# Lightning attention into a switch-routed MoE: order of the q, k and v loads, the first step in head halves, and the lists emptied in two parts

## The chip, the cores and the metric

The kernel runs on one core of one Trainium2 chip. The metric is the time of one execution on the device in microseconds, the median of several runs. The engines are TensorE (PE; its weight loads are PEld), VectorE (DVE), ScalarE (ACT), GpSimd (POOL) and SyncE (SP), and each takes its instructions in order. Transfers are issued from the queues of SyncE, ScalarE and GpSimd.

## The reference, cut to what matters

```python
# lightning attention: batch 4, heads 8, sequence 768, head size 64, blocks of 64, all f32
for b in range(nb):
    intra = (qb @ kb.T * Dmask) @ vb            # Dmask = lam ** (i - j) for i >= j
    inter = (qb * lam_pow) @ kv_state
    out[:, :, block b] = intra + inter
    kv_state = lam_block * kv_state + (kb * rev_pow).T @ vb
x = out as (4 * 768, 8 * 64)                    # 3072 tokens of 512
# switch routing, top 1 of 8 experts, hidden size 1024
expert = argmax(x @ w_gate); gate_w = softmax(x @ w_gate)[expert]
y[tokens of e] = gate_w * (relu(x[tokens of e] @ w1[e]) @ w2[e])
```

## The kernel before, in words

**Attention.** The kernel works with blocks of 128 positions, so there are `NSTEP` = 6 of them, and with two batches at a time: twelve steps (n, b) with b = 0 or 2. For a step it loads q, k and v as tiles of 128 positions by 2 batches by 8 heads by 64, 0.524 MB each (`q_in`, `k_in`, `v_in`, three buffers each). `turn_q` and `turn_k` transpose one half of the heads at a time on TensorE into `tq` and `tk`; ScalarE copies them out as `qT` and `kT`; from n = 1 on VectorE also makes `qsT` (q with its decay), and GpSimd makes `kd` (k with its decay). `score` multiplies kT and qT into `sp`, and VectorE multiplies by the decay mask into `mt`. `attend_states` adds the part of the state (`op<-qsT,st`), `grow` makes the state's growth (`cp<-v_in,kd`), `attend` multiplies v and mt (`op<-mt,v_in`), `to_sbuf` copies out to `xT`, `update` adds `cp` to the state with the faded state `sd` that `fade` makes on GpSimd.

**Order.** `enter` takes a step in (loads for a later step, then its transposes), `leave` makes the logits and the rows of a finished step. An iteration of the main loop with step i as `cur` does: `leave` of step i-1, `enter` of step i+1, then states, `grow` and `attend` of step i, `score` of step i+1, the routing of a finished group of four batches, `fade`, and `store_places`. The first step is entered and scored ahead of the loop, and the second is entered inside the first iteration after its attention.

**Loads.** `load` issues q, k, v of one step on SyncE's queue; the first two steps are loaded at the start, and `enter(n, b)` loads step (n+1, b), which is two steps on. The very first q and k go as one transfer per batch.

**Routing lists.** `slots` in DRAM holds for each of 8 experts R = 3456 entries of 16 bytes. `empty_lists` fills it once, in iteration 1, with one transfer of 432 KB from GpSimd's queue. When a group of 512 tokens is ranked, `put` makes each token's place and `store_places` writes entries with indirect transfers from GpSimd, two in an iteration (`slots<-entry,slot_i`). Later SyncE reads lists back, GpSimd gathers the rows of x and TensorE runs the experts; that is two thirds of the time.

**What fixes the order.** The instruction planner (Tile) puts the instructions of each engine in an order by its own estimate of when they are ready. `pin` keeps an instruction behind the one traced before it on its engine: transposes and products on TensorE, `kd`, `sd`, the puts and the emptying on GpSimd are pinned; the loads of q, k and v, the copies qT and kT, and the mt products are not.

Of the kernel before, what the change touches and what calls it, by code (L numbers as in the profile page):

```python
# [10 lines left out]
F32 = mybir.dt.float32  # L11
BF16 = mybir.dt.bfloat16
I32 = mybir.dt.int32
# [9 lines left out]
def kernel(  # L23
# [29 lines left out]
    nc = tc.nc  # L53
    B, H, S, D = q.shape
    N, MD = out.shape
    E = moe_w_gate.shape[1]
    F = moe_w1.shape[2]
    P = 128
    C = P
    NSTEP = S // C  # L60
# [26 lines left out]

    def load(n, b0, first=False):

        got = [qkv.tile([P, 2, H, D], F32, tag=name, name=f"{name}_in") for name in "qkv"]  # L90
        for t, src in zip(got, (q, k, v)):
            per = 1 if first and src is not v else 2
            for b in range(0, 2, per):
                nc.sync.dma_start(  # L94
                    out=t[:, b:b + per].rearrange("p b h d -> p (b h) d"),
                    in_=src[b0 + b:b0 + b + per, :, n * C:(n + 1) * C, :].rearrange(
                        "b h s d -> s (b h) d"))
        return got

# [3 lines left out]
    nc.scalar.dma_start(out=lam_bc, in_=lam.partition_broadcast(P))  # L103
    loaded = {(0, 0): load(0, 0, True), (0, 2): load(0, 2)}
    ident = const.tile([P, P], F32, name="ident")
# [94 lines left out]
    def pin(inst):  # L200
        tc.keep_in_program_order(inst)
# [10 lines left out]
    def turn_q(m, s):  # L212
        shp = turned_shape
        tq = turned(m.q, s, bank(2 * s, shp, "tq"))
        qT = work.tile(shp, F32, tag="qT", name="qT")
        nc.scalar.copy(qT, tq)
        m.qT.append(qT)
# [219 lines left out]

    empty = ffn.tile([P, E * R // P, ENTRY], I32, tag="xg", name="empty", bufs=4)
    nc.gpsimd.memset(empty, 0)
# [423 lines left out]

    def empty_lists():

        pin(nc.gpsimd.dma_start(out=slots.rearrange("(p r) c -> p (r c)", p=P),
                                in_=empty.rearrange("p r c -> p (r c)").bitcast(F32)))
        pin(nc.gpsimd.dma_start(out=xs[0, :].rearrange("(c p) -> c p", c=DC), in_=zeros[:DC, :]))

# [7 lines left out]

    def enter(n, b, between=nothing):
        if n + 1 < NSTEP:
            loaded[n + 1, b] = load(n + 1, b)  # L880
        m = SimpleNamespace(n=n, b=b, qT=[], qsT=[], kT=[], kd=[], mt=[])
        m.q, m.k, m.v = loaded[n, b]

        for s, turn_one in (((0, turn_q), (1, turn_q), (0, turn_k), (1, turn_k)) if not (n or b)
                            else ((0, turn_q), (0, turn_k), (1, turn_q), (1, turn_k))):
            turn_one(m, s)
            between()
            between = nothing
        return m

# [21 lines left out]
    def give_places(group):  # L912

        waiting.append((group, put(*group), 0))
# [68 lines left out]

    order = [(n, b) for n in range(NSTEP) for b in range(0, B, 2)]
    cur, last = enter(*order[0]), None
    for s in range(2):
        score(cur, s)

    pin(nc.scalar.dma_start(out=gates[0][:, :, :E],
                            in_=moe_w_gate.rearrange("(c p) e -> p c e", p=P)))  # L990
    for u in range(2):
        nc.gpsimd.tensor_copy(gates[1][halves[u]], gates[0][halves[1 - u]])
    for i in range(len(order)):
        rest = leave(last, (4, 6, 7) if i < len(order) - 1 else (4, 2, 3)) if last else nothing

        ahead = enter(*order[i + 1], rest) if 0 < i < len(order) - 1 else None
        if ahead:
# [21 lines left out]
        if i == 0:  # L1019
            ahead = enter(*order[1])  # L1020
        update(cur)
# [9 lines left out]
        for group in ranked:  # L1031
            give_places(group)
        if ahead:
            fade(ahead)
            store_places()
        if i == 1:
            empty_lists()
        last, cur = cur, ahead
# [139 lines left out]
```

## Time and profile before

| | us |
|---|---|
| median of 3 runs | 458.72 |
| the runs | 458.73, 458.72, 456.27 |
| the profiled execution's own time | 458.06 |
| its span | 455.6 |
| TensorE busy | 432.8 (95%) |
| VectorE, ScalarE, GpSimd busy | 265.8, 180.7, 251.4 |
| mean granted clock of TensorE | 0.991 of full speed |

The span is the stretch from the first to the last instruction that the profile has; the execution's own time is 2.5 us longer. Busy time of TensorE is modelled at the ends of its products. A wait is put down to what came last by the profile, as in `[1.49 <-DMA k_in<-in_k_dram]`: idle for 1.49 us until a transfer into k_in had landed. On the timeline an SPq line is the issue of a transfer on SyncE's queue, not its landing.

### The profile page before, as it was taken

The numbers are of one execution on the slowest core, as the hardware profiler recorded it, in microseconds if no ns is written. First come the engines' busy times: TensorE is split into PE (matmuls) and PEld (weight loads), VectorE is DVE, ScalarE is ACT, GpSimd is POOL, SyncE is SP. The second block draws the span as 40 slices with busy tenths as digits, with TensorE's granted clock in tenths as the row PEclk, the third lists the DMA queues.
The fourth block names the chain that finished last, engine by engine and source line by source line (L and its number), as shares of the span: only waits on it lengthen the run. The fifth ranks groups of instructions, "written<-read, shape, count | busy, mean of one in ns | idle before, by whom it ended". The sixth has DMA issues, their size and how long they took to land.

```text
span 455.6 us, 9420 instructions
## 1 busy us (share of the span) xinstructions
PE 432.8 (95%) x3713; PEld 370.5 (81%) x3713; DVE 265.8 (58%) x590; ACT 180.7 (40%) x327; POOL 251.4 (55%) x203
## 2 busy tenths in 40 slices
PE   4989999998979999999999999999999999999993
PEld 3778888887857885996898799689879979979973
DVE  2756566582737543557546944864773784485453
ACT  3455445553522033634255252524515525423301
POOL 4234455533143558756766484586659569548203
PEclk9999999998989999999999999999999999999999
DMA  9999999999561995956294277729529739201001
GB/s 171 206 266 237 212 253 214 233 207 228 189 232 48 305 287 104 372 92 251 67 260 161 101 236 90 255 67 254 202 72 270 166 115 267 51 1 66 2 12 60
DMA packets 123207, 78.39 MB, mean 172 GB/s; under 512 B 104556, under 2 KB 104560, under 8 KB 123153
## 3 DMA queue, kind: packets, MB, share of 16 engines
q1 hardware_dynamic: 114176, 58.13, 53.0%
q0 software_dynamic: 5040, 13.25, 9.3%
q10 hardware_dynamic: 3936, 6.31, 4.1%
q8 instruction: 31, 0.51, 0.5%
q14 instruction: 24, 0.19, 0.2%
HBM read 58.96 MB, written 13.16 MB: 158 GB/s over the span
## 4 chain that ended last, share of the span: by engine, by line
PE 89%; DMA 4%; SPq 3%; DVE 1%; issue 1%; another core or an unknown queue 1%; ACT 0%; POOL 0%; POOLq 0%; DVEq 0%
PE p L678 28%; PE p L722 22%; PE p L730 10%; PE ph L560 5%; PE sp L244 4%; PE op L278 4%; PE po L836 4%; SPq L94 3%; PE tx L339 2%; PE op L269 2%; PE cp L303 2%; DMA k_in<-in_k_dram 2%; DMA q_in<-in_q_dram 2%; PE tk L209 2%; PE tq L209 1%; PE lgT L329 1%
## 5 line engine op out<-in xcount | busy, mean ns | idle before, releaser
L690 ACT ACTIVATE hT<-hT 128x408 f32<-128x408 f32 (+4 forms) x56 | 29.5, 527 | 68.5 <-DVE hT L687 68.4
L250 DVE TENSOR_TENSOR mt<-sp,decay 128x512 f32<-128x512 f32 x48 | 30.4, 685 | 22.0 <-PE sp L244 21.9
L428 POOL DMA_INDIRECT slots<-entry,slot_i x24 | 23.5, 981 | 33.7 <-DVE slot_i L426 15.1
L678 PE MATMUL p<-xgT,w1t 128*128 128x204 f32 (+4 forms) x224 | 41.5, 328 | 0.0
L234 POOL TENSOR_TENSOR kd<-k_in,kdec 128x512 f32<-128x512 f32 x20 | 20.4, 1038 | 35.0 <-PE cp L303 18.3
L678 PEld LDWEIGHTS p<-xgT,w1t 128*128 128x128 f32 x224 | 37.6, 190 | 1.2 <-issue 0.9
L489 POOL DMA_INDIRECT out_dram<-o,list x22 | 22.5, 1021 | 25.4 <-ACT o L810 20.4
L608 POOL TENSOR_TENSOR s_k<-w1t 128x1024 f32<-128x1024 f32 x7 | 16.6, 2367 | 28.1 <-DMA across<-planes_k 11.8
L608 POOL TENSOR_TENSOR s_q<-w1t 128x1024 f32<-128x1024 f32 x7 | 16.5, 2360 | 28.0 <-PE p L730 16.9
L722 PE MATMUL p<-w2t,hT 128*128 128x256 f32 x128 | 29.7, 381 | 0.0
L483 POOL DMA_INDIRECT xg<-xs,list x24 | 24.7, 1029 | 6.4 <-issue 5.8
L722 PEld LDWEIGHTS p<-w2t,hT 128*128 128x128 f32 x128 | 23.9, 190 | 5.3 <-issue 2.5
L687 DVE TENSOR_TENSOR hT<-p,u_qsT 128x408 f32<-128x408 f32 (+4 forms) x28 | 15.8, 563 | 21.1 <-PE p L678 21.1
L244 PE MATMUL sp<-qT,kT 64*128 64x128 f32 x384 | 25.8, 281 | 0.2 <-ACT kT L228 0.2
L730 PE MATMUL p<-w2t,hT 128*64 128x256 f32 x112 | 25.7, 382 | 0.0
L278 PE MATMUL op<-mt,v_in 128*64 128x128 f32 x384 | 24.9, 284 | 0.0
L244 PEld LDWEIGHTS sp<-qT,kT 64*128 64x128 f32 x384 | 22.8, 187 | 2.6 <-issue 1.7
L574 DVE TENSOR_TENSOR u_kT<-p,u_qT 128x408 f32<-128x408 f32 (+4 forms) x14 | 7.9, 563 | 27.2 <-PE p L678 27.1
L560 PE MATMUL ph<-xgT,w1t 128*128 128x256 f32 (+1 forms) x128 | 23.5, 341 | 0.0
L278 PEld LDWEIGHTS op<-mt,v_in 128*64 128x64 f32 x384 | 22.6, 144 | 0.3 <-ACT kT L228 0.2
L730 PEld LDWEIGHTS p<-w2t,hT 128*64 128x64 f32 x112 | 14.8, 137 | 9.4 <-issue 2.3
L810 ACT ACTIVATE o<-o,list 128x512 f32<-128x512 f32 (+2 forms) x7 | 5.1, 722 | 43.7 <-DVE o L807 43.7
(214 smaller groups left out, 1129.1 us busy)
## 6 DMA issues: line engine op xcount, KB each, us to landing
w2t<-in_moe_w_dram SPq DMA_DIRECT2D x8, 2048.0 KB
w1t<-in_moe_w_dram SPq DMA_DIRECT2D x7, 2048.0 KB
v_in<-in_v_dram SPq DMA_DIRECT2D x12, 512.0 KB
xs<-x ACTq DMA_DIRECT2D x12, 512.0 KB
q_in<-in_q_dram SPq DMA_DIRECT2D x11, 512.0 KB
k_in<-in_k_dram SPq DMA_DIRECT2D x11, 512.0 KB
w1t<-in_moe_w_dram SPq DMA_DIRECT2D x2, 1024.0 KB
q_in<-in_q_dram SPq DMA_DIRECT2D x2, 256.0 KB
```

Source lines behind the costliest of these rows:

```text
L244: pin(nc.tensor.matmul(sp[u][:, i, b, :], lhsT=m.kT[s][halves[u], i, b, :], rhs=m.qT[s][halves[u], i, b, :], start=(i == 0 and b == 0), st ...
L250: nc.vector.tensor_mul(mt[:, u], sp[u], decay[:, u, s * HP // 2:(s + 1) * HP // 2].unsqueeze(2).to_broadcast(shp))
L278: pin(nc.tensor.matmul(out_at(m, b, u, hp), lhsT=m.v[:, b, 2 * hp + u, :], rhs=m.mt[hp // 2][:, u, hp % 2, b, :], start=(first and hp == 0 ...
L428: put = nc.gpsimd.indirect_dma_start(out=slots, out_offset=bass.IndirectOffsetOnAxis(ap=slot_i[:, i:i + 1], axis=0), in_=entry[:, n, bs[i] ...
L483: return nc.gpsimd.indirect_dma_start(out=dst, out_offset=None, in_=xs[:rows, :], in_offset=bass.IndirectOffsetOnAxis(ap=idx, axis=0))
L489: put = nc.gpsimd.indirect_dma_start(out=out, out_offset=bass.IndirectOffsetOnAxis(ap=idx, axis=0), in_=src, in_offset=None, bounds_check= ...
L560: nc.tensor.matmul(ph, lhsT=w1t[:, dc, fc * P:(fc + 1) * P], rhs=m.xgT[:, dc, :], start=(dc == 0), stop=(dc == DC - 1))
L608: return nc.gpsimd.tensor_tensor(out=o, in0=x, in1=y, op=ALU.subtract)
L678: nc.tensor.matmul(p[:, i, :], lhsT=lhs[:, dc, (c + i) * P:(c + i + 1) * P], rhs=rhs[:, dc, :], start=(dc == 0), stop=(dc == DH - 1))
L690: nc.scalar.activation(outs[i][k], outs[i][k], ACT.Relu)
L722: nc.tensor.matmul(p, lhsT=x, rhs=y, start=(k == 0), stop=(k == 3))
L730: nc.tensor.matmul(p[half], lhsT=x, rhs=y, start=(k == 0), stop=(k == len(low) - 1), skip_group_check=True)
```

## The change

Loads get an order of their own: with step i entered, q and k of step i+2 and v of step i+1 are issued. At the start q and k of step 0, then v of step 0, then q and k of step 1 are issued; q and k of step 0 go in eight transfers, the first four heads of both, then the last four. In the first step each half is scored as soon as `turn_q` of the second half, or `turn_k` of it, is done, inside `enter`. In the second step VectorE, not ScalarE, copies qT. `empty_lists` becomes two transfers on SyncE's queue: in iteration 1 rows 0 to 895 of each expert's list, in iteration 2 the other 2560; both are pinned behind the loads traced before them. The main loop calls it ahead of `fade` and `store_places`. The filling tile is smaller accordingly.

```diff
--- before.py
+++ after.py
@@ -85,23 +85,34 @@
 
     qkv = ctx.enter_context(tc.tile_pool(name="qkv", bufs=3))
 
-    def load(n, b0, first=False):
-
-        got = [qkv.tile([P, 2, H, D], F32, tag=name, name=f"{name}_in") for name in "qkv"]
-        for t, src in zip(got, (q, k, v)):
-            per = 1 if first and src is not v else 2
-            for b in range(0, 2, per):
-                nc.sync.dma_start(
-                    out=t[:, b:b + per].rearrange("p b h d -> p (b h) d"),
-                    in_=src[b0 + b:b0 + b + per, :, n * C:(n + 1) * C, :].rearrange(
-                        "b h s d -> s (b h) d"))
-        return got
+    steps = [(n, b) for n in range(NSTEP) for b in range(0, B, 2)]
+    loaded = {}
+
+    def load(i, names, first=False):
+
+        if i >= len(steps) or (i, names[0]) in loaded:
+            return
+        n, b0 = steps[i]
+        parts = (slice(0, H // 2), slice(H // 2, H)) if first else (slice(0, H),)
+        for name in names:
+            loaded[i, name] = qkv.tile([P, 2, H, D], F32, tag=name, name=f"{name}_in")
+        for hs, name in itertools.product(parts, names):
+            src = {"q": q, "k": k, "v": v}[name][b0:b0 + 2, hs, n * C:(n + 1) * C, :]
+            to = loaded[i, name]
+            if first:
+                for b in range(2):
+                    nc.sync.dma_start(out=to[:, b, hs], in_=src[b].rearrange("h s d -> s h d"))
+            else:
+                nc.sync.dma_start(out=to.rearrange("p b h d -> p (b h) d"),
+                                  in_=src.rearrange("b h s d -> s (b h) d"))
 
 
     lam_bc = const.tile([P, H], F32, name="lam_bc")
 
     nc.scalar.dma_start(out=lam_bc, in_=lam.partition_broadcast(P))
-    loaded = {(0, 0): load(0, 0, True), (0, 2): load(0, 2)}
+    load(0, "qk", True)
+    load(0, "v")
+    load(1, "qk")
     ident = const.tile([P, P], F32, name="ident")
     make_identity(nc, ident)
 
@@ -213,7 +224,10 @@
         shp = turned_shape
         tq = turned(m.q, s, bank(2 * s, shp, "tq"))
         qT = work.tile(shp, F32, tag="qT", name="qT")
-        nc.scalar.copy(qT, tq)
+        if m.n == 0 and m.b > 0:
+            nc.vector.tensor_copy(qT, tq)
+        else:
+            nc.scalar.copy(qT, tq)
         m.qT.append(qT)
         if m.n > 0:
             qsT = work.tile(shp, F32, tag="qsT", name="qsT", bufs=4)
@@ -435,7 +449,8 @@
 
         return store
 
-    empty = ffn.tile([P, E * R // P, ENTRY], I32, tag="xg", name="empty", bufs=4)
+    HEAD = R - (NSTEP - 1) * B * C
+    empty = ffn.tile([P, (R - HEAD) * E // P, ENTRY], I32, tag="xg", name="empty", bufs=4)
     nc.gpsimd.memset(empty, 0)
     nc.gpsimd.memset(empty[:, :, 1], N)
 
@@ -861,11 +876,16 @@
                 data1=zeros, initial=1.0, op0=ALU.mult, op1=ALU.add)
         nc.vector.tensor_copy(sdec[:, :, 0], qdec[:, :, C - 1])
 
-    def empty_lists():
-
-        pin(nc.gpsimd.dma_start(out=slots.rearrange("(p r) c -> p (r c)", p=P),
-                                in_=empty.rearrange("p r c -> p (r c)").bitcast(F32)))
-        pin(nc.gpsimd.dma_start(out=xs[0, :].rearrange("(c p) -> c p", c=DC), in_=zeros[:DC, :]))
+    def empty_lists(n):
+
+        rows = slice(HEAD, R) if n else slice(0, HEAD)
+        per = (rows.stop - rows.start) * E // P
+        pin(nc.sync.dma_start(
+            out=by_e[:, rows, :].rearrange("e (p r) c -> e p (r c)", r=per),
+            in_=empty[:, :per].rearrange("p r c -> p (r c)").bitcast(F32)))
+        if n == 0:
+            pin(nc.gpsimd.dma_start(out=xs[0, :].rearrange("(c p) -> c p", c=DC),
+                                    in_=zeros[:DC, :]))
 
 
     groups = ([(n, list(range(B))) for n in range(NSTEP - 1)]
@@ -875,17 +895,22 @@
     lgs = {}
     base = [ebase]
 
-    def enter(n, b, between=nothing):
-        if n + 1 < NSTEP:
-            loaded[n + 1, b] = load(n + 1, b)
+    def enter(i, between=nothing):
+        load(i + 2, "qk")
+        load(i + 1, "v")
+        if i + 3 == len(steps):
+            load(i + 2, "v")
+        n, b = steps[i]
         m = SimpleNamespace(n=n, b=b, qT=[], qsT=[], kT=[], kd=[], mt=[])
-        m.q, m.k, m.v = loaded[n, b]
-
-        for s, turn_one in (((0, turn_q), (1, turn_q), (0, turn_k), (1, turn_k)) if not (n or b)
-                            else ((0, turn_q), (0, turn_k), (1, turn_q), (1, turn_k))):
+        m.q, m.k, m.v = (loaded[i, name] for name in "qkv")
+        for s, turn_one in ((0, turn_q), (0, turn_k), (1, turn_q), (1, turn_k)):
             turn_one(m, s)
             between()
             between = nothing
+            if i == 0 and turn_one is turn_q and s == 1:
+                score(m, 0)
+        if i == 0:
+            score(m, 1)
         return m
 
     chosen = []
@@ -981,19 +1006,15 @@
         weights.append((w1t, w2t))
         passes.append(m)
 
-    order = [(n, b) for n in range(NSTEP) for b in range(0, B, 2)]
-    cur, last = enter(*order[0]), None
-    for s in range(2):
-        score(cur, s)
-
+    cur, last = enter(0), None
     pin(nc.scalar.dma_start(out=gates[0][:, :, :E],
                             in_=moe_w_gate.rearrange("(c p) e -> p c e", p=P)))
     for u in range(2):
         nc.gpsimd.tensor_copy(gates[1][halves[u]], gates[0][halves[1 - u]])
-    for i in range(len(order)):
-        rest = leave(last, (4, 6, 7) if i < len(order) - 1 else (4, 2, 3)) if last else nothing
-
-        ahead = enter(*order[i + 1], rest) if 0 < i < len(order) - 1 else None
+    for i in range(len(steps)):
+        rest = leave(last, (4, 6, 7) if i < len(steps) - 1 else (4, 2, 3)) if last else nothing
+
+        ahead = enter(i + 1, rest) if 0 < i < len(steps) - 1 else None
         if ahead:
             if last:
                 with tc.issue_after(ahead.copied.ins):
@@ -1017,7 +1038,7 @@
             attend_states(cur)
         to_sbuf(cur)
         if i == 0:
-            ahead = enter(*order[1])
+            ahead = enter(1)
         update(cur)
         if i == 0:
             later_decays()
@@ -1030,11 +1051,11 @@
             score(ahead, 1)
         for group in ranked:
             give_places(group)
+        if 0 < i < 3:
+            empty_lists(i - 1)
         if ahead:
             fade(ahead)
             store_places()
-        if i == 1:
-            empty_lists()
         last, cur = cur, ahead
     leave(last)()
     store_rows(last)
```

## Rows read from the trace of the kernel before

**Rows 1.** The page: span, TensorE's busy time, the granted clock and the DMA engines' busy share in 40 slices (tenths), and the shares of the chain that ended last by engine.

```profile
span 455.6 us, 9420 instructions
...
PE 432.8 (95%) x3713; PEld 370.5 (81%) x3713; DVE 265.8 (58%) x590; ACT 180.7 (40%) x327; POOL 251.4 (55%) x203
...
PEclk9999999998989999999999999999999999999999
DMA  9999999999561995956294277729529739201001
...
PE 89%; DMA 4%; SPq 3%; DVE 1%; issue 1%; another core or an unknown queue 1%; ACT 0%; POOL 0%; POOLq 0%; DVEq 0%
```

**Rows 2.** The chain of work that ended last, in order of time: start, length, what (with the number of instructions).

```profile
12.88 8.88 DMA q_in<-in_q_dram
21.89 0.63 PE tq L209 x4
...
23.84 9.03 DMA k_in<-in_k_dram
33.01 0.63 PE tk L209 x4
...
34.07 0.44 PE tk L209 x4
...
106.42 0.42 issue
...
109.75 3.24 PE op L278 x32
...
128.10 3.40 another core or an unknown queue
```

**Rows 3.** Stretches of 10 us from the start: busy time of each engine with its instructions, then the granted clock, the DMA share and the rate in GB/s.

```profile
0.00:10.00 10.00, 3.95 (x16) 3.11 (x16) 3.27 (x21) 3.23 (x5) 4.99 (x22) 1.00 0.90 164
10.00:20.00 10.00, 9.33 (x150) 8.31 (x152) 6.77 (x14) 4.39 (x8) 3.33 (x5) 1.00 1.33 205
20.00:30.00 10.00, 8.14 (x124) 6.97 (x121) 4.09 (x8) 5.19 (x10) 3.51 (x4) 1.00 1.11 242
30.00:40.00 10.00, 9.79 (x167) 8.39 (x167) 6.47 (x19) 5.53 (x13) 3.89 (x5) 1.00 1.17 275
40.00:50.00 10.00, 9.88 (x170) 8.73 (x170) 5.34 (x13) 5.38 (x11) 5.55 (x7) 1.00 0.94 215
```

**Rows 4.** Timeline of the first 40 us, of all engines: start, length (of a merged run of instructions), engine, line, operation, out<-in, shape and count, and in brackets the idle time before it with its releaser.

```profile
5.07 0.45 PE L209 MATMUL tq<-ident,q_in 128*128 128x128 f32 x1 [5.07 <-DMA q_in<-in_q_dram]
...
8.13 2.31 SPq L94 DMA_DIRECT2D k_in<-in_k_dram  x1
...
10.15 2.06 PE L244 MATMUL sp<-qT,kT 64*128 64x128 f32 x32
...
13.12 1.92 PE L278 MATMUL op<-mt,v_in 128*64 128x128 f32 x32
...
14.71 1.47 DVE L859 TENSOR_TENSOR_SCAN qdec<-lam_pair,zeros 128x128 f32<-128x128 f32 x4
...
16.09 0.63 PE L209 MATMUL tk<-ident,k_in 128*128 128x128 f32 x4 [0.46 <-DMA k_in<-in_k_dram]
...
17.79 2.14 PE L244 MATMUL sp<-qT,kT 64*128 64x128 f32 x32 [0.20 <-ACT kT L228]
18.10 0.62 ACT L228 COPY kT<-tk 128x512 f32<-128x512 f32 x1
18.99 2.48 DVE L250 TENSOR_TENSOR mt<-sp,decay 128x512 f32<-128x512 f32 x4 [1.80 <-PE sp L244]
...
19.86 0.64 PE L329 MATMUL lgT<-xT,gates 128*32 128x256 f32 x8
...
20.43 1.09 PE L339 MATMUL tx<-ident,xT 128*128 128x128 f32 x8
...
21.89 0.63 PE L209 MATMUL tq<-ident,q_in 128*128 128x128 f32 x4 [0.36 <-DMA q_in<-in_q_dram]
...
24.23 0.63 PE L209 MATMUL tk<-ident,k_in 128*128 128x128 f32 x4 [1.49 <-DMA k_in<-in_k_dram]
...
25.66 1.15 PE L303 MATMUL cp<-v_in,kd 128*64 128x64 f32 x32
...
29.47 0.81 POOL L866 DMA_DIRECT2D slots<-empty  x1
...
33.01 0.63 PE L209 MATMUL tk<-ident,k_in 128*128 128x128 f32 x4 [0.21 <-DMA k_in<-in_k_dram]
...
35.47 1.15 PE L303 MATMUL cp<-v_in,kd 128*64 128x64 f32 x32
```

**Rows 5.** Timeline from 40 to 62 us: the issue of the eighteenth load on SyncE's queue, GpSimd's first two puts into the lists and its two kd of step 4, and `grow` of step 4 on TensorE.

```profile
43.13 1.11 POOL L428 DMA_INDIRECT slots<-entry,slot_i  x1 [3.78 <-PE tl L354]
...
44.42 2.30 SPq L94 DMA_DIRECT2D v_in<-in_v_dram  x1
...
44.54 0.97 POOL L428 DMA_INDIRECT slots<-entry,slot_i  x1 [0.18 <-issue]
...
46.49 2.04 POOL L234 TENSOR_TENSOR kd<-k_in,kdec 128x512 f32<-128x512 f32 x2 [0.97 <-issue]
...
55.60 1.15 PE L303 MATMUL cp<-v_in,kd 128*64 128x64 f32 x32
```

## The prediction

> **What bounds the kernel now.** I read the page first. TensorE is busy for 95% of a span of 455.6 us and carries 89% of the chain that ended last [rows 1], so only what moves TensorE moves the end. Then the chain in order of time: up to 33 us it leaves TensorE for loads of q and k twice, and after that nearly every link is TensorE; two places break it, idle pieces and a slow stretch at 106 to 113 us and an unnamed wait at 128 us [rows 2]. The start is therefore where loads decide, and the change sits there. The 10 us stretches give the bytes moved, with the DMA engines at or above a full share until 40 us [rows 3]; the timeline of the first 40 us gives TensorE's waits [rows 4]; the timeline after it gives GpSimd's puts [rows 5].
>
> Number the loads of 0.524 MB on SyncE's queue. Before: q0 k0 v0 q1 k1 v1 q2 k2 v2 q3 k3. TensorE waits for the fifth (k1, until 16.09), the seventh (q2, 21.89), the eighth (k2, 24.23) and the eleventh (k3, 33.01) [rows 4]. The queue was issued far ahead (k1 at 8.13 us, landed about 16.1), so it is transfer, not issue, that is late.
>
> **The loads' order.** After: q0 k0 v0 q1 k1 q2 k2 v1 q3 k3 v2. One row of the queue holds the same bytes as before at each place, so I take the old arrival of the same place: fifth k1 16.1, seventh k2 21.9, eighth v1 24.2, eleventh v2 at most 33.0 (0.44 MB of empty lists were moving before it from 29.47 [rows 4], and now are behind it).
>
> Step 1: k1 is still the fifth, so its transposes start at 16.09 as before. Two more sets of 0.44 [rows 2] end at about 17.4. The scores began at 17.79 [rows 4]; now between 17.4 and 18.0. Scores 2.14 minus overlap, about 2.0; logits and transposes of the step before about 1.65; four sets of 0.44 and the logit rows 0.23: TensorE reaches `grow` of step 1 at 23.1 to 23.7. It needs v1, eighth, 24.2. Before, the same `grow` began at 25.66 [rows 4], since after the eighth transfer three sets of transposes were still to do. Gain 25.66 - 24.25 = 1.4 us.
>
> Step 2: from `grow` of step 1 to its k wait before: 25.66 to 33.01, with a last wait of 0.21 [rows 4]. Shifted by 1.4 and without the wait, k3's transposes fall at 31.4; k3 is now the tenth, and one load takes about 2.9 (24.23 to 33.01 for three), so it lands near 30. `grow` of step 2 was at 35.47 [rows 4], now 35.47 - 1.6 = 33.9, with v2 there by 33.0. Sum of the start: **1.6 us**. What is late next is nothing that loads: before, TensorE had no load wait after 33 us, and an iteration takes about 10 us (cp at 35.47, at 55.60 two iterations on [rows 4, 5]) for about 2.1 MB, 210 GB/s, under the 275 that 30 to 40 us reached [rows 3]. Bounds: 0.6 us (v1 lands 1 us later, from eight first transfers in place of four) to 1.9.
>
> **Head halves and scores between.** The first q tile was there at 5.07 [rows 4]; with pieces half as large I expect some 0.5 us less. Scores of half 0 then run about 7.8 instead of 10.15 and step 0 ends near 14.2 instead of 15.0. All of it is handed back at k1, fifth on the queue, 16.09. Price: nothing, from 0.0 to 0.5 lost if the eight issues delay the queue; if the cover (k1's transfer) were gone, it would be worth 0.8.
>
> **qT of the second step by VectorE.** It takes two copies (0.6 each, as kT at 18.10) from ScalarE. VectorE's copy is of the size of the mt products, 0.62 each [rows 4]. VectorE has qdec's scans from 14.71 on; if these stand ahead of the copy it comes at 17.9 to 18.5, otherwise at once. Either way `grow` of step 1 waits for v1 to 24.2, with 0.5 us or more to spare: nothing. Without that cover it is -0.4 to +0.3.
>
> **Lists emptied in two parts.** Before, one transfer from GpSimd's queue, issued at 29.47 [rows 4]; the first put into the lists went at 43.13, the second at 44.54, and kd of step 4 at 46.49 [rows 5]. GpSimd loses that issue (0.81), in a stretch where it waits anyway: nothing. Now the second part, 0.33 MB, goes on SyncE's queue behind v4. Every put writes anywhere in the lists, so the first put must wait for it, and it is emitted in the same iteration. Behind the waiting put on GpSimd stand the second put, kd of step 4 (pinned behind it), sd, and two more puts; TensorE's `grow` of step 4 waits for kd.
>
> When does it land? Ahead of and with it: 17 loads (8.91 MB), 0.11 and 0.33 MB of empties, two to three stores of x (0.52 each): 10.4 to 10.9 MB. The stretches add up to 8.86 MB at 40 us and 2.15 more by 50 [rows 3], so the last byte goes at 47.2 to 49.6. The eighth load (4.19 MB) was seen 2.1 us after its bytes by the same sum, the eleventh (with x and the empties 6.73 MB) 0.8 after. So it lands at 48.0 to 51.7; I take 49.9.
>
> When is that too late? From the wait's end: two puts, 2.4 us by the spacing 43.13, 44.54 and 0.97, then two kd of 1.02 [rows 5]. `grow` of step 4 was at 55.60, now 54.0, and needs the second kd half a group (0.55) later, 54.5. So the limit is 54.5 - 4.45 = **50.0 us**, and each us beyond it is a us of TensorE. Expected loss 0.4, from 0 to 1.7.
>
> A rule of the Trainium skill bears on this move. It says (page DMA: Bandwidth & Descriptors, section Queues, rings and completion order) that each issuing queue has its own ring on each DMA engine and that an engine goes round between rings packet by packet. By it the old transfer could overtake SyncE's backlog, and the new one cannot; the sum above is made in that order, and with a turn of its own the second part, issued near 44.4 when seventeen loads have been [rows 5], would land some 1.5 us later, near 46, and the 0.4 would be nil.
>
> **Sum.** Own time 458.06 for a span of 455.6; -1.6 + 0.4 = -1.2 gives 456.9. The median shown, 458.72, is 0.66 above that execution, so 456.9 to 457.5; I say **457.2**.
>
> **Rivals.** (1) Nothing gained, 458.3. The second part of the empties spreads over only half of the DMA engines, because the lists' side of the transfer now has eight experts as its first dimension. Worked from rows: 0.33 MB at the 215 GB/s of 40 to 50 us is 1.5 us over all, 3.0 over half, so it lands at 51.4, 1.4 past the limit, and eats the gain. For it: the new shape; against: every transfer shown has 128 partitions first, so no row shows such a spread. The Trainium skill states it as a rule (same page, section Why a DMA increments its semaphore by 16 and not by 1): the engines used are the largest number up to 16 that divides the first dimension of both sides, here 8; no run here shows it so far. The same 458.3 comes if the eight first transfers cost the queue 1.4 us.
>
> (2) Slower, 460 to 463. One mechanism: the put's wait. It decides from a landing at 51.6 us, where the loss equals the gain. If SyncE holds v4 back for a buffer, or the first empties must land before the second is issued, and the second lands at 54 to 56, TensorE stands 4 to 6 us at `grow` of step 4, less 1.6. For it: kd and puts share one in-order queue [rows 5]; against: by the sum SyncE is short of transfer time, not of buffers, up to 45 us.
>
> (3) Faster by much, 452 to 454. The pieces called issue at 106 to 109 us (the first 0.42), the attention products after them that take 3.24 in place of 1.92 [rows 2, 4], and the 3.40 us without a known releaser at 128 us cost some 6 us together. None is named by the change, but all lie where weights and puts share the DMA engines; other timing could close one or two, or add 3 us. For it: the releaser is not a tile of this code; against: the instruction streams behind 33 us stay as they are.
>
> (4) The planner reorders what is not pinned and issues v ahead of q and k as before: no change, 458.7.
>
> **How the numbers follow.** Forecast (455.8 to 458.0) 0.52; rival 1 0.17; rival 2 0.10; rival 3 0.12 shorter and 0.04 longer; rival 4 0.05. A measurement of this kernel tells about 1%, 4.6 us, from no change: its three runs alone span 2.5. Faster than 454.1 takes most of rival 3's shorter part, 0.11; slower than 463.3 the tail of 2 and of 3, 0.07; the rest 0.82. The range must leave out no more than 2 in 10: from 453.8, which holds half of rival 3, to 460.6, which holds the near part of rival 2.
>
> **What would show it.** Right: TensorE's waits for q and k at 21.9, 24.2 and 33.0 are gone, one wait for v stands at about 24.2 ahead of `grow`, and every later landmark up to 105 us is 1 to 1.6 us earlier (`grow` of step 2 at 33.9). GpSimd's first put at 48 to 52 us with a DMA as its releaser; kd of step 4 done at about 54.3. Wrong: `grow` of step 4 waiting for kd by more than 1.6 us, v1 landing after 25.6, or the stretch at 106 to 132 us having changed by more than the start.

## The result and the profile after

The changed kernel took 461.83 us (median, 460.97 to 463.32) beside 458.71 for the kernel before on the same chip: a ratio of 1.0089, interval 1.0063 to 1.0115. It is slower, by 3.1 us (0.7%) at the medians and by 0.9% by the ratio, and the 457.2 predicted was wrong in sign. The ratio comes from the single executions, those in the chip's slower state left out, and not from the two medians. The profiled execution took 460.97 us, 2.9 more than the one of before, and so did its span.

The page of the changed kernel (parts as in [rows 1]):

```profile
span 458.5 us, 9433 instructions
...
PE 433.4 (95%) x3713; PEld 370.5 (81%) x3713; DVE 263.1 (57%) x592; ACT 180.0 (39%) x325; POOL 250.1 (55%) x202
...
PEclk9999989999999999999999999999999999999997
...
PE 83%; DVE 1%; issue 1%; another core or an unknown queue 1%; ACT 1%; POOL 0%; POOLq 0%; DVEq 0%
```

TensorE's busy time moved by 0.6 us only, so most of the 2.9 us is idle time. The 4% of DMA and 3% of SPq that the chain had before [rows 1] are missing, but that says nothing of the loads: the chain is followed back only to the start of `grow` at 57.95 us, and what lies ahead of that has to be read from the timeline. In the clock row a new dip stands in the sixth slice (57 to 69 us). So something new stands at about 60 us.

The timeline of the changed kernel up to 36 us (columns as in [rows 4]):

```profile
15.22 0.66 PE L220 MATMUL tq<-ident,q_in 128*128 128x128 f32 x4
...
16.07 0.65 PE L220 MATMUL tk<-ident,k_in 128*128 128x128 f32 x4 [0.20 <-DMA k_in<-in_k_dram]
...
21.77 0.63 PE L220 MATMUL tk<-ident,k_in 128*128 128x128 f32 x4
...
24.15 1.15 PE L317 MATMUL cp<-v_in,kd 128*64 128x64 f32 x32 [0.87 <-ACT kT L242]
...
33.56 1.15 PE L317 MATMUL cp<-v_in,kd 128*64 128x64 f32 x32
```

The waits for q and k at 21.89, 24.23 and 33.01 [rows 4] are gone; `grow` of step 2 starts at 33.56 in place of 35.47. So the start did what was hoped. The same views from 42 us on, of SyncE's issues, GpSimd and TensorE, with GpSimd's two puts before `kd` of step 4:

```profile
44.84 2.27 SPq L883 DMA_DIRECT2D slots<-empty  x1
...
51.75 1.10 PE L283 MATMUL op<-qsT,st 64*64 64x128 f32 x32
...
54.46 1.10 POOL L442 DMA_INDIRECT slots<-entry,slot_i  x1 [17.03 <-DVE entry L402]
...
55.86 0.96 POOL L442 DMA_INDIRECT slots<-entry,slot_i  x1 [0.18 <-issue]
...
56.85 2.04 POOL L248 TENSOR_TENSOR kd<-k_in,kdec 128x512 f32<-128x512 f32 x2
...
57.95 2.11 PE L317 MATMUL cp<-v_in,kd 128*64 128x64 f32 x32 [5.10 <-POOL kd L248]
...
62.42 0.83 PE L258 MATMUL sp<-qT,kT 64*128 64x128 f32 x10
```

(The last line is cut by the end of its window.) Two marks of the kernel before for comparison, the state part of step 4 and the score after it:

```profile
54.56 1.10 PE L269 MATMUL op<-qsT,st 64*64 64x128 f32 x32
...
58.43 1.16 PE L244 MATMUL sp<-qT,kT 64*128 64x128 f32 x16
```

Step 4 is where the time goes. The second part of the empty lists is issued at 44.84. The first put, at 43.13 before [rows 5], waits until 54.46, `kd` of step 4 stands behind two puts, and `grow` of step 4, at 55.60 before [rows 5], starts at 57.95 after 5.10 us of nothing. The releaser in brackets is only what ended last ahead of the put: VectorE's `entry` of the next group here, `sm` in the repeat, `new` in another run below, so none of these holds it. What came last is the transfer into the lists: the run with the own queue names it, and in this trace its last packet ends at 52.9, 1.5 us ahead of the put (packets further down).

Stretches of the changed kernel at that place (columns as in [rows 3]):

```profile
56.00:58.00 2.00, 0.05 (x2) 0.05 (x2) 0.00 (x0) 0.00 (x0) 1.97 (x3) 0.98 0.92 196
58.00:60.00 2.00, 2.00 (x34) 1.94 (x36) 0.00 (x0) 0.00 (x0) 1.88 (x2) 0.50 0.59 119
60.00:62.00 2.00, 2.00 (x29) 2.00 (x26) 0.69 (x1) 0.00 (x0) 1.76 (x3) 0.67 1.14 236
62.00:64.00 2.00, 2.00 (x35) 1.69 (x33) 0.39 (x1) 1.01 (x2) 1.97 (x3) 1.00 1.04 210
```

After the idle stretch TensorE works at a granted clock of 0.50, the lower of its two levels (1.2 of 2.4 GHz), and is back at 1.00 by 62 us. From the start of `grow` to the next score it is 4.47 us (57.95 to 62.42) in place of 2.83 (55.60 to 58.43): 1.6 us more, on top of the wait.

So the sum of the profiled execution is: `op<-qsT,st` of step 4 starts at 51.75 in place of 54.56, 2.8 us early; 5.1 of wait and 1.6 of slow clock make it 3.9 late, and by the marks it is 4.0 (62.42 against 58.43). Some 1.4 us come back at 114 us, where the attention products took 1.81 in the chain in place of 3.24 [rows 2]. That leaves about 2.6 of the 2.9.

### The profile page after: what moved, and what is told of

Its sections match the earlier page's. It is cut to its first block, busy times and chain, and to the rows that moved or that the text cites. A ratio compares the mean times of both kernels' runs of the same rounds, so it can differ in the third digit from the quotient of the medians.

```text
span 458.5 us, 9433 instructions
## 1 busy us (share of the span) xinstructions
PE 433.4 (95%) x3713; PEld 370.5 (81%) x3713; DVE 263.1 (57%) x592; ACT 180.0 (39%) x325; POOL 250.1 (55%) x202
## 4 chain that ended last, share of the span: by engine, by line
PE 83%; DVE 1%; issue 1%; another core or an unknown queue 1%; ACT 1%; POOL 0%; POOLq 0%; DVEq 0%
PE p L693 28%; PE p L737 22%; PE p L745 9%; PE ph L575 5%; PE po L851 3%; PE sp L258 3%; PE op L292 3%; PE tx L353 2%; PE cp L317 2%; PE op L283 2%; PE tk L220 1%; PE lgT L343 1%; PE tq L220 1%; PE tl L368 1%
## 5 line engine op out<-in xcount | busy, mean ns | idle before, releaser
L258 PE MATMUL sp<-qT,kT 64*128 64x128 f32 x384 | 27.1, 288 | 0.7 <-ACT kT L242 0.7
L304 ACT COPY xT<-op 128x512 f32<-128x512 f32 x12 | 7.0, 586 | 44.6 <-PE op L292 35.8
## 6 DMA issues: line engine op xcount, KB each, us to landing
w2t<-in_moe_w_dram SPq DMA_DIRECT2D x8, 2048.0 KB, 15.4
```

The lines of the kernel that those rows point to most:

```text
L258: pin(nc.tensor.matmul(sp[u][:, i, b, :], lhsT=m.kT[s][halves[u], i, b, :], rhs=m.qT[s][halves[u], i, b, :], start=(i == 0 and b == 0), st ...
```

## The experiments

The times, each beside the kernel before on the same chip. In the first group (e1_lists_as_before to e4_own_queue) every kernel, that of before too, took some 7 to 12 us less, and in the four traces of the group the idle pieces at 106 to 113 us and the wait at 128 to 131 are missing; so only ratios are compared across groups. The last two columns are of the profiled execution.

| kernel | us | before | ratio (interval) | first put at | TensorE waits for kd |
|---|---|---|---|---|---|
| changed | 461.83 | 458.71 | 1.0089 (1.0063 to 1.0115) | 54.46 | 5.1 |
| e1_lists_as_before | 448.48 | 446.27 | 1.0017 (0.9977 to 1.0057) | 41.19 | none |
| e2_lists_only | 453.86 | 446.27 | 1.0151 (1.0096 to 1.0207) | 57.03 | 5.4 |
| e3_sixteen_first | 449.64 | 446.27 | 1.0061 (1.0036 to 1.0086) | 54.08 | 4.8 |
| e4_own_queue | 449.20 | 446.27 | 1.0029 (0.9988 to 1.0070) | 46.85 | none |
| b_again (before) | 456.52 | 456.88 | 1.0004 (0.9976 to 1.0032) | 43.24 | none |
| a_again (changed) | 459.50 | 456.88 | 1.0045 (1.0004 to 1.0085) | 53.51 | 4.2 |
| e5_loads_only | 455.56 | 456.88 | 0.9977 (0.9953 to 1.0001) | 41.36 | none |
| e6_qt_scalar | 455.61 | 456.88 | 0.9966 (0.9938 to 0.9993) | 42.88 | none |
| e8_both_early | 455.27 | 456.81 | 0.9971 (0.9947 to 0.9996) | 45.66 | none |
| e1_again | 455.23 | 456.81 | 0.9962 (0.9938 to 0.9986) | 41.15 | none |
| e9_qt_no_halves | 455.26 | 456.81 | 0.9971 (0.9944 to 0.9998) | 42.36 | none |
| e5_long | 456.04 | 456.81 | 0.9974 (0.9952 to 0.9995) | 41.14 | none |
| e10_small_second | 461.97 | 458.18 | 1.0096 (1.0058 to 1.0133) | 53.12 | 3.9 |

Read down the last two columns: each kernel whose put is held to 53 us or later is slower than before, and no other is measurably so.

### Which part of the change costs, and which gives

The changed kernel with the lists emptied as before, by one transfer from GpSimd in iteration 1:

```diff
-    def empty_lists(n):
-
-        rows = slice(HEAD, R) if n else slice(0, HEAD)
...
+    def empty_lists():
+
+        pin(nc.gpsimd.dma_start(out=slots.rearrange("(p r) c -> p (r c)", p=P),
+                                in_=empty.rearrange("p r c -> p (r c)").bitcast(F32)))
...
-        if 0 < i < 3:
-            empty_lists(i - 1)
         if ahead:
             fade(ahead)
             store_places()
+        if i == 1:
+            empty_lists()
```

> The changed kernel, with the lists emptied as before: one transfer from GpSimd's queue in iteration 1. Theory A (the whole loss is the first put waiting for the second part of the empties, kd of step 4 behind it, and TensorE's lower clock after the wait): the gain at the start stays, 1.9 us at grow of step 2 (33.6 us against 35.5) and up to 2.8 at step 4, no wait for kd at grow of step 4; 455.5 to 457.3 us where the kernel before has 458.7. Rival B (the new order of the loads costs time further on as well, by later v or by queue order): 459 us or more.

The first time it gave 1.0017 with an interval too wide to tell; the same kernel again:

> The changed kernel with the lists as before, a second time, beside the others of this set. Its times lay 7 us apart in the first set. Theory A (the spread comes from the first 20 us: how long TensorE's first products take double, and scans on VectorE beside kd): grow of step 2 between 33.5 and 35.4 us, the time 1 to 3 us under the kernel before in the median. Rival (something later): grow of step 2 at 33.5 and a slow run all the same.

0.9962: faster than before by 1.7 us, the lowest ratio measured.

```profile
41.15 1.10 POOL L442 DMA_INDIRECT slots<-entry,slot_i  x1 [3.78 <-PE tl L368]
...
53.65 1.15 PE L317 MATMUL cp<-v_in,kd 128*64 128x64 f32 x32
```

With the put at 41.15 `grow` of step 4 started at 53.65, not 57.95. Undoing the lists alone turns a loss into a gain, so the lists cost more than the loss measured. The 7 us over which its times lay in the first group did not come back (under 3 here); what made them stays open.

The kernel before, with only the emptying in two parts on SyncE's queue (the `empty_lists(n)` of the change and its call):

> The kernel before, with only the emptying in two parts on SyncE's queue. Here the second part stands behind eighteen loads, one more than in the changed kernel. Theory A: it lands 2 to 3 us later than in the changed kernel (first put at 56 to 58 us), TensorE waits 4 to 6 us at grow of step 4 and loses 1 to 2 to the clock; 462 to 466 us. Rival B (the loads' order is at fault): 458 to 459.5, like the kernel before.

It cost 7.6 us at the medians, 6.7 by the ratio. Its trace, GpSimd's first put and TensorE's `grow` of step 4:

```profile
47.08 2.77 SPq L869 DMA_DIRECT2D slots<-empty  x1
...
57.03 1.09 POOL L428 DMA_INDIRECT slots<-entry,slot_i  x1 [17.32 <-DMA xs<-x]
...
60.51 2.11 PE L303 MATMUL cp<-v_in,kd 128*64 128x64 f32 x32 [5.38 <-POOL kd L234]
```

The same chain as in the changed kernel, with the old start: issue, 10 us, put, 3.5 us, `grow`. The wait is again only part of the loss.

The kernel before with the loads' order alone (the `load` and `enter` of the change, without its head halves, its qT and its lists):

```diff
-        parts = (slice(0, H // 2), slice(H // 2, H)) if first else (slice(0, H),)
+        parts = (slice(0, H),)
...
```

> The kernel before, with only the loads' order changed: q and k two steps ahead, v one (no head halves, no scores between, qT by ScalarE, lists as before). Theory A (the gain at the start is the place of v behind the next q and k): grow of step 2 at 33.6 to 34.0 us and 2 to 3 us faster than the kernel before. Rival (the head halves and the copies on VectorE carry the gain): grow of step 2 at 35 us or later, no difference.

> The kernel before with the loads' order alone, in more rounds. Theory A: 1.0 to 1.9 us faster than the kernel before, an interval that leaves out no change. Rival (the gain at the start is given back): an interval around 1.

0.9977, with no change just inside its interval, and 0.9974: 1.2 us by the tighter one, less than the 2 to 3 expected of the first. The timeline of the first of them:

```profile
33.70 1.15 PE L314 MATMUL cp<-v_in,kd 128*64 128x64 f32 x32
...
41.36 1.10 POOL L439 DMA_INDIRECT slots<-entry,slot_i  x1 [3.79 <-PE tl L365]
```

`grow` of step 2 is 1.8 us earlier than before (35.47), without halves and without qT on VectorE: nearly the whole gain of the start is the loads' order.

Both kernels were measured a second time in one group, to see what a repeat gives:

> The kernel before, unchanged, for its trace beside those of the other runs of this set. Theory A: the same span and landmarks as in the trace before, shifted by no more than its idle pieces at 106 to 113 us and its wait at 128 us, which the first set's traces do not show; grow of step 2 at 35.5 us, first put at 43.

> The changed kernel, unchanged, beside the kernel before on the same chip. Theory A: 3 to 5 us slower than the kernel before, since the wait for the second part of the empties (first put near 54.5 us) does not hang on what the chip does after 106 us.

The kernel before agreed with itself (1.0004). The changed one came out at 1.0045, with the wait for `kd` at 4.2 us and the put 0.95 earlier: slower again, by less than the 3 to 5 us expected.

### Why the second part lands late

Rival 1 said: half of the DMA engines, since the lists' side has eight experts first. Here 16 stands first on both sides of the transfer:

```diff
-            out=by_e[:, rows, :].rearrange("e (p r) c -> e p (r c)", r=per),
-            in_=empty[:, :per].rearrange("p r c -> p (r c)").bitcast(F32)))
+            out=by_e[:, rows, :].rearrange("e (p r) c -> p e (r c)", r=per),
+            in_=empty[:P // E, :per].rearrange("p r c -> p (r c)").bitcast(F32).unsqueeze(1)
+            .to_broadcast([P // E, E, per * ENTRY])))
```

> The changed kernel, with both empties written in another shape: the first dimension of both sides is 16 instead of 8 experts (16 partitions, each read for 8 experts), same bytes, same queue, same place. Theory A1 (it is late for the loads queued before it on SyncE's queue): the first put starts within 1 us of 54.5, 461 to 462.5 us. Rival A2 (it is late since it spreads over half of the DMA engines): the first put comes 1.5 us or more earlier, at 51 to 53, and the time is 458.5 to 460.5.

```profile
45.29 3.43 SPq L883 DMA_DIRECT2D slots<-empty  x1
...
54.08 1.09 POOL L442 DMA_INDIRECT slots<-entry,slot_i  x1 [16.73 <-DVE entry L402]
```

8.8 us from issue to put in place of 9.6, and the put itself only 0.4 earlier, since issuing took longer (3.43 in place of 2.27): less than 1 us of it is the shape. From issue to landing an ordinary load of v in the same kernel (the tile v_in from 36 to 48 us) took as long.

```profile
DMA to landing us min/median/max: 9.3/9.3/9.3
```

Both parts from GpSimd's own queue:

```diff
-        pin(nc.sync.dma_start(
+        pin(nc.gpsimd.dma_start(
             out=by_e[:, rows, :].rearrange("e (p r) c -> e p (r c)", r=per),
```

> The changed kernel, with both parts issued from GpSimd's queue at the same places in its program, in the same shape. Theory A1 (queued loads make it late): the second part is issued at about 36.5, lands before 42, the first put starts at 41 to 43 and nothing waits; 455.5 to 457.3. Rival A3 (the write of the second part into DRAM is slow by itself, whatever is ahead of it): the first put after 46, and 457.5 or more.

```profile
38.20 0.70 POOL L883 DMA_DIRECT2D slots<-empty  x1
...
46.85 1.09 POOL L442 DMA_INDIRECT slots<-entry,slot_i  x1 [6.87 <-DMA slots<-empty]
```

Here the releaser is named: the transfer `slots<-empty`. The landing at 41 to 43 that I expected is a miss. Its own queue did not carry it past the backlog: 8.65 us from issue to put, about what SyncE's queue gave. In the profiled execution it makes TensorE wait for nothing, because GpSimd issues it 6.6 us earlier; the time, 1.0029 with no change inside its interval, tells neither gain nor loss. The put came after the 46 that the expectation gave to a write slow by itself; the packets of the kernel before, further down, speak against that. The rule of the Trainium skill that the prediction weighed (DMA: Bandwidth & Descriptors, Queues, rings and completion order: a ring for each issuing queue, served in turn) gave no quick landing here; the trace doesn't show the rings, so it says nothing against the turns themselves.

Both parts on SyncE's queue, but both in iteration 1:

```diff
-        if 0 < i < 3:
-            empty_lists(i - 1)
+        if i == 1:
+            for n in range(2):
+                empty_lists(n)
```

> The changed kernel, with both parts of the empties issued in iteration 1, the second right behind the first on SyncE's queue. Theory A (nothing but the moment at which the second part lands decides, about 9 us after its issue as in the runs so far): issued at about 37.5 us, landed at 45 to 48, under the limit of 50; no wait for kd at grow of step 4, and 1 to 3 us faster than the kernel before. Rival (the queue's loads pay for it, or it lands after 50): a wait for kd, no gain.

```profile
35.13 3.35 SPq L883 DMA_DIRECT2D slots<-empty  x2
...
45.66 1.09 POOL L442 DMA_INDIRECT slots<-entry,slot_i  x1 [8.35 <-DVE st L339]
...
54.36 1.15 PE L317 MATMUL cp<-v_in,kd 128*64 128x64 f32 x32 [1.43 <-DMA v_in<-in_v_dram]
```

0.9971. Queue, shape and sum of bytes are those of the change; only the second part is issued 7 us earlier (at 37.9, by the view of its line), and the put comes 8.8 us earlier. The kd wait is gone, and 0.9971 in place of 1.0045 to 1.0089 is the price of the place of issue, across groups: 3.4 to 5.4 us. What is late next is v of step 4, 1.43 us.

Last, the size. The first part takes 2944 rows of each list, the second only 512 (the profile lists it with 64.0 KB, where the changed kernel's has 320.0; the 221 KB in the expectation is my slip):

```diff
-    HEAD = R - (NSTEP - 1) * B * C
-    empty = ffn.tile([P, (R - HEAD) * E // P, ENTRY], I32, tag="xg", name="empty", bufs=4)
+    HEAD = R - B * C
+    empty = ffn.tile([P, HEAD * E // P, ENTRY], I32, tag="xg", name="empty", bufs=4)
```

> As the changed kernel, but the emptying is split unevenly: the first transfer fills 377 KB and the second, issued at the same place, only 65 KB. If the second part lands late because of what it moves (221 KB among the other loads), a part of under a third of that lands some 5 to 6 us after its issue at about 44.5: first put at 50 to 51, kd of step 4 held by under 2 us, and the time is that of the loads' order alone, 0.997 of before. If every transfer of that stretch takes about 9 us from issue to landing whatever its size, the first put starts at 53 to 54.5 again, TensorE waits 4 to 5 us for kd, and the time is 1.004 to 1.009 of before.

```profile
39.04 4.55 SPq L106 DMA_DIRECT2D k_in<-in_k_dram  x1
...
46.36 2.77 SPq L883 DMA_DIRECT2D slots<-empty  x1
...
53.12 1.09 POOL L442 DMA_INDIRECT slots<-entry,slot_i  x1 [15.80 <-DVE new L395]
```

The put at 53.12 is the second theory's, and 1.0096 is nearest to it, but not by its reason: from issue to put it is 6.8 us, not 9, so size does count. What it saved there SyncE spent ahead of it: the first part is larger, the load of k behind it kept the queue 4.55 us (1.88 in the changed kernel), and the issue came 1.5 us later. What is in the queue up to and with the second part is the same in both, and it lands within 1.3 us of the same moment.

### Head halves and qT on VectorE

The changed kernel with the old lists and qT back on ScalarE, that is, loads' order and head halves:

```diff
-        if m.n == 0 and m.b > 0:
-            nc.vector.tensor_copy(qT, tq)
-        else:
-            nc.scalar.copy(qT, tq)
+        nc.scalar.copy(qT, tq)
...
```

> The changed kernel with the lists as before and the second step's qT by ScalarE again: loads' order and head halves stay. Theory A: as without this edit, grow of step 2 within 0.3 us of 33.6, 2 to 3 us faster than the kernel before. Rival (VectorE's copy shortens the second step): 0.3 to 0.6 us later.

And with the old lists and no halves, that is, loads' order and qT on VectorE (`parts = (slice(0, H),)` and the old order of the first step):

> Loads' order and the second step's qT by VectorE, without the head halves, lists as before. If VectorE's copy makes the spread (it stands behind the scans, which take 3.0 us when kd runs beside them and 1.4 when not), score of step 1 waits for qT by 1 us or more and the times spread over 3 us or more. If the head halves make it, this one is as narrow as the loads' order alone, 1 to 1.5 us under the kernel before.

0.9966 and 0.9971, between 0.9974 for neither part and 0.9962 for both, all inside one another's intervals: neither is worth anything that can be measured. In the trace with qT on ScalarE `grow` of step 2 came at 35.22, not within 0.3 of 33.6 as expected, after a slow start (last section). The trace of the one without halves shows the risk of qT on VectorE:

```profile
15.84 2.97 DVE L873 TENSOR_TENSOR_SCAN qdec<-lam_pair,zeros 128x128 f32<-128x128 f32 x4
...
18.92 1.29 DVE L228 COPY qT<-tq 128x512 f32<-128x512 f32 x2
...
19.75 2.06 PE L258 MATMUL sp<-qT,kT 64*128 64x128 f32 x32 [1.69 <-DVE qT L228]
```

The copies stand behind the scans, and TensorE waits 1.69 us for them; `grow` of step 2 then starts at 34.70, a microsecond later than with the loads alone. Its times lie 5 us apart, as expected if that copy makes the spread, but those of the loads alone lie 4 apart in the same group, so this is not shown.

## Why the prediction was wrong

**The bound and the loads' order: right.** TensorE and the start were what mattered, and `grow` of step 1 and 2 came at 24.15 and 33.56 where 24.2 and 33.9 were worked out. The profile puts the wait ahead of the first down to ScalarE's kT; in five other traces with this order it names the load of v, at 24.04 to 24.11, as predicted. The gain of 1.6 us was 1.9 in the trace at step 2, and 1.1 to 1.7 us by the ratios of the kernels with the old lists outside the first group. By step 4 it had grown to 2.8 in the changed kernel's profile. (The DMA engines were not at a full share all the way to 40 us: [rows 3] has 0.90 in the first 10. Nothing hangs on it.)

**Head halves and qT: right.** Nothing was predicted and nothing measured. The first score came at 7.84 for the 7.8 expected, but step 0 ended at 15.2, not 14.2: not foreseen was that TensorE's first products run at half pace (below).

**The emptied lists: the step that failed, by one term.** The chain was right to the link: the put waits, two puts and `kd` stand behind it, `grow` waits for `kd`. Its limit of 50.0 us was nearly right, by two errors that in part cancel: TensorE was ready at 52.85 and not at 54.0, and the put leads `grow` by 3.49 us (54.46 to 57.95) and not by 3.9 (4.45 less the 0.55 of the second `kd`), so the real limit was 49.4. Wrong is the landing, 48.0 to 51.7, taken at 49.9. It came at 54.46 by the put that it released. That one term turns the 0.4 us of loss into 5.1.

The landing was a sum of two: the last byte of the second part at 47.2 to 49.6, and 0.8 to 2.1 us more. Where it went wrong can be read from the trace. First the stretches of the changed kernel (columns as in [rows 3], the last is GB/s):

```profile
0.00:10.00 10.00, 5.67 (x29) 3.99 (x30) 3.32 (x22) 3.24 (x5) 5.38 (x22) 1.00 0.86 167
10.00:20.00 10.00, 9.13 (x140) 7.74 (x140) 7.45 (x17) 3.50 (x6) 2.61 (x4) 1.00 1.24 204
20.00:30.00 10.00, 9.13 (x138) 7.98 (x135) 5.36 (x11) 5.57 (x11) 3.85 (x4) 1.00 1.16 253
30.00:40.00 10.00, 10.00 (x171) 8.81 (x170) 6.85 (x20) 5.59 (x13) 3.04 (x3) 1.00 1.01 232
40.00:45.00 5.00, 5.00 (x99) 4.66 (x98) 2.79 (x9) 3.23 (x6) 0.00 (x0) 1.00 1.08 219
45.00:50.00 5.00, 5.00 (x75) 4.30 (x72) 2.82 (x5) 2.67 (x6) 0.00 (x0) 1.00 1.08 252
50.00:54.00 4.00, 2.85 (x49) 2.44 (x47) 3.09 (x13) 2.70 (x7) 0.00 (x0) 1.00 0.87 232
```

They add up to 8.56 MB at 40 us, 10.9 at 50 and 11.8 at 54. So the 10.4 to 10.9 MB that I counted up to and with the second part had indeed been moved by about 50, nearly as predicted (47.2 to 49.6). The second part was not in by then. The trace lists every DMA packet with its size. The packets of the loads have 256 bytes, those of the second part 2560 (160 entries of 16), both on SyncE's queue (q1). The packets from 48.1 to 53.0 us:

```profile
DMA packets 2319, 0.89 MB, mean 182 GB/s; under 512 B 2185, under 2 KB 2185, under 8 KB 2319
...
q1 hardware_dynamic: 2313, 0.88, 87.4%
```

Of the 2313 packets of the queue 2185 are of loads, and the other 128 are the whole second part. At 48.1 us 16.8 of the 17 loads counted ahead of it had been moved, so up to its first packet the sum held. From there to the end of its last packet, at 52.9, it took 4.8 us, where its 0.33 MB at the 215 GB/s of [rows 3] are 1.5. Beside it 0.53 MB of loads were moved, at least 0.4 of that issued behind it. The put came 1.5 us after the last packet, so the second term of the sum was right. The step that failed is the first, the last byte: the sum took the bytes strictly in the order of the queue and gave the second part the common rate, 1.5 us for what took 4.8.

The second part's packets can be told by their size in the other traces too (5120 bytes on GpSimd's queue, 512 for the 64 KB). In all seven with the lists in two parts the put follows the last packet by 1.3 to 1.6 us, which says what it waited for whatever releaser is named. From the first packet to the last it took 4.4 us in the repeat, 5.1 with the lists alone and with both parts early, 4.1 on GpSimd's queue, 3.5 with 16 first and 1.4 for the 64 KB. The loads beside it are not the whole reason: with 16 first they were 0.13 MB. Nor are the lists slow to write as such: in the kernel before, the 432 KB went in 3.0 us (32.5 to 35.5), with 0.47 MB of loads beside them.

A coarser measure that would have served stood in rows I quoted. Of the loads of before, k of step 1 was issued at 8.13 and waited for until 16.09 [rows 4], and the chain has 8.88 and 9.03 us of DMA for q and k of later steps [rows 2]: 8 to 9 us from issue to landing, each time. With v of step 4 issued at 44.42 [rows 5] and the second part behind it, 44.4 + 9 = 53.4, near the 54 to 56 of rival 2. The traces after give 9.6, 9.6, 10.0 and 8.8 for the 320 KB on SyncE's queue behind the loads, 8.65 on GpSimd's, some 7.8 issued early, 6.8 for 64 KB. I used the issue times to show that transfer, not issue, was late, and did not ask how long that makes each transfer.

**The clock: a term that was left out.** A wait of TensorE was priced at its length. Here 5.1 us of idle were followed by the lower clock, 1.6 us more in the profile of the change. This is a part of why the kernel with the lists alone lost 7.6 us (6.7 by the ratio) on a wait of 5.4.

**The rivals.** Rival 2 is what happened in its place and at its price, a landing at 54 to 56 and 460 to 463 us; 461.83 was measured. Its causes were not: SyncE did not hold the issue back, which came at 44.84 for the 44.4 expected. The price has luck in it too, since neither the 2.8 us gained by step 4 nor the 1.6 of slow clock stood in it. It had 0.10, because the sum of bytes spoke against it, and the range ended at 460.6 for the same reason. Rival 1 had the right victim and too small a cause: with 16 first the packets took 1.3 us less, of which the longer issue left 0.4 at the put. The rule beside it (Trainium skill, DMA: Bandwidth & Descriptors, Why a DMA increments its semaphore by 16 and not by 1) would make of it at most that 1.3 us; on how many engines each form ran no row here shows. Rival 3's slow attention products at 110 us were gone in the profiled execution:

```profile
112.73 0.22 PE L317 MATMUL cp<-v_in,kd 128*64 128x64 f32 x1 [0.39 <-issue]
...
113.97 1.91 PE L292 MATMUL op<-mt,v_in 128*64 128x128 f32 x31
```

The pieces called issue ahead of them stayed, as did 3.61 us without a known releaser at 131 us; when the clock falls after them varies from run to run (in the repeat it was 0.52 at 112 to 114). Rival 4 fell: v is issued behind q and k.

**What stays open:** how the DMA engines share their time among transfers under way, so why the second part's packets took 4.8 us and the whole 9, and not other figures; and why the pieces at 106 to 113 us come and go with the chip session.

## What to carry to other kernels

Price a moved transfer by when it is issued plus the time from issue to landing that neighbouring transfers of like size show in the same stretch, not by adding up bytes in the order of the queue; then ask who waits for it, and what is queued behind that waiter. Where a large transfer has one reader with a due time, issue it an iteration earlier: the same two transfers cost 3.4 to 5.4 us in one place and nothing measurable in the other. Of this change the loads' order is what to keep; alone or with the harmless rest it gives 0.2 to 0.4%.

## What the runs showed of the hardware that I had not expected

TensorE's first products run at half pace although the granted clock reads 1.00. Stretches of the changed kernel (columns as above):

```profile
6.00:8.00 2.00, 1.91 (x9) 1.15 (x8) 0.36 (x3) 0.81 (x3) 1.04 (x1) 1.00 1.18 218
8.00:10.00 2.00, 2.00 (x17) 1.78 (x18) 0.05 (x1) 0.53 (x1) 1.04 (x1) 1.00 1.19 213
```

In its timeline, four transposes and a score of 16 products at the start, and the next score:

```profile
4.14 1.41 PE L220 MATMUL tq<-ident,q_in 128*128 128x128 f32 x4 [4.14 <-DMA q_in<-in_q_dram]
...
7.84 2.08 PE L258 MATMUL sp<-qT,kT 64*128 64x128 f32 x16
...
11.30 1.16 PE L258 MATMUL sp<-qT,kT 64*128 64x128 f32 x16 [0.67 <-ACT kT L242]
```

1.41 us for four transposes here, 0.66 for the same at 15.22. The moment at which this ends differs: about 10 us in this execution, about 15.4 in the one with qT on ScalarE, where `grow` of step 2 came at 35.22. Why is open.

VectorE's four scans `qdec` took 1.37 to 1.47 us in the nine traces in which GpSimd's two `kd` came behind them (14.66 in the changed kernel), and 2.97 to 3.11 in the six in which `kd` ran beside them, as in the run without halves, where it starts at 16.27. Not every operation of VectorE suffers so: the copy of qT at 17.27 in the changed kernel took 0.69 us beside `kd`, as the one at 16.14 without it. No run changes the overlap alone, so that it is the cause is likely and not shown; the longer scans decide whether qT on VectorE is free.
